# A small marker transfer that holds back one key load in a DMA-bound attention decode kernel

## The chip, the cores and the metric

One core of a Trainium2 chip. The metric is the device time of the whole program in microseconds (us), the median of several executions. The core was alone. A "ratio" below is worked out from runs of the same rounds, so it isn't quite the ratio of the medians that stand beside it. "Span" is the length of the one profiled execution, about 2 us shorter than its device time.

## The reference

Two attention layers, A and B, decode one token for four batch entries; their results are concatenated.

```python
# per layer: x (4, 1, 512), caches (4, 8, 8192, 128), wq (512, 4096), wo (4096, 512), bf16
q = (x @ wq) -> (4, 32, 1, 128)
k, v = caches, each of 8 heads used by 4 query heads   # B: only the last 2048 tokens
p = softmax(q k^T * 128 ** -0.5)
layer = (p v) -> (4, 1, 4096) @ wo
out = concatenate([A, B], axis=-1)                     # (4, 1, 1024)
```

## The kernel before

The work is cut into 20 units: four of layer B and sixteen of layer A (two heads of one batch entry each). An A unit loads 4 MB of keys and 4 MB of values into one of two slots, transposes the keys on TensorE, computes scores, the softmax and the weighted sum. From unit 6 on, every second unit also brings in 1 MB of the output weights, called a piece. SyncE issues all these loads, each behind the wait that frees its buffer. The part that matters (cuts are marked with ...):

```python
def kv_load(kind, u):
    ...
    w = [("otr", u - 2)] if kind == "V" else [("otr", u - 3)] if u >= 2 * T0P else [("T", tjob_idx[(u - 2, NJ - 1)])]
    ...
    op("sp", lambda sp: sp.sem_inc(sem, bump), waits=w, bump=(sem, bump, None))
    ...
    op("sp", dma(buf[:, slot, :, :].rearrange("p t d -> p (t d)"), src), inc=(kind, u, 0))
...
for u in range(1, NU + 1):
    if u < NU:
        kv_load("K", u)
    kv_load("V", u - 1)
    tn = u // 2
    if u % 2 == 0 and tn in pieces:
        P, q = pieces[tn]
        src = WO[P][q * C * DH:(q + 1) * C * DH, :].rearrange("(p r) n -> p (r n)", p=128)
        op("sp", dma(Wo_sb[:, :, :].rearrange("p r n -> p (r n)"), src), waits=[("ocp", tn - 1)], inc=("wo", tn))
```

So the order around the first piece is: keys of unit 6, values of unit 5, the piece, keys of unit 7, values of unit 6, keys of unit 8.

## Time and profile before

| | before |
|---|---|
| median device time | 439.15 us (3 runs, 438.97 to 439.83) |
| span of the profiled run | 437.0 us |
| bytes read | 184.56 MB |
| TensorE busy | 365.0 us (84%) |
| share of the 16 DMA engines' time in SyncE's queue | 99.1% |

The first thing to read is which resource has no free time. That is the DMA queue; the lines stand in the prediction. The second is what each of the sixteen DMA engines does by itself, and no single line of the page says that. I took it from the completion increments in the trace: a transfer over 128 partitions leaves sixteen of them, one per engine. In the text below, an engine's "lead" is how long before the last engine it finished the same transfer, "spread" is the greatest lead, a "straggler" is one engine well behind all others, and "lands" means the last increment. The profile doesn't number the engines: that two packets ran on the same one is read from the second starting where the first ends.

### The profile page before, as it was taken

Reading aid. Unit: us, or ns where it says so; the run is one execution under the profiler, and the core shown is the slowest. Engines: PE = TensorE matmul, PEld = TensorE weight load, DVE = VectorE, ACT = ScalarE, POOL = GpSimd, SP = SyncE. Lnnn points to the kernel's source line nnn. Section 1 sums busy time; section 2 is a strip of 40 time slices with the busy share of each in tenths; the row PEclk is TensorE's granted clock in tenths of the full one; section 3 lists DMA queues with packets and bytes.
Section 4 is the critical chain, followed back from the end, with each engine's and each line's share of the span. In section 5 each row is a group of like instructions: output and inputs, shape, how many; then the busy total and the mean of one; then the engine's idle time right before and its main releaser. Section 6 shows DMA issues by size and latency. Waiting matters only on the chain.

```text
span 437.0 us, 15525 instructions
## 1 busy us (share of the span) xinstructions
PE 365.0 (84%) x7174; PEld 337.9 (77%) x7184; DVE 210.0 (48%) x406; ACT 195.0 (45%) x249; POOL 27.7 (6%) x88
## 2 busy tenths in 40 slices
PE   0168898998998959895989598969868996989996
PEld 0158897997997949795979588868868886979975
DVE  0004455664564634563456247525643563455651
ACT  1024473573653625371634254434534462536530
POOL 6100000000000000000000000000100000000000
PEclk9999999999999988999999899989996999799999
DMA  8999999999999999999999999999999999999996
GB/s 340 430 421 421 429 412 430 418 439 412 445 432 432 424 438 432 432 432 432 432 432 429 432 432 430 431 433 432 410 454 432 432 432 432 432 432 411 447 407 255
DMA packets 10996, 184.73 MB, mean 423 GB/s; under 512 B 1236, under 2 KB 2280, under 8 KB 2408
## 3 DMA queue, kind: packets, MB, share of 16 engines
q1 hardware_dynamic: 10960, 184.56, 99.1%
q8 instruction: 8, 0.13, 0.1%
q14 instruction: 4, 0.03, 0.0%
q10 hardware_dynamic: 24, 0.01, 0.0%
HBM read 184.56 MB, written 0.01 MB: 422 GB/s over the span
## 4 chain that ended last, share of the span: by engine, by line
PE 54%; DMA 40%; issue 2%; DVE 1%; SPq 1%; ACT 1%
DMA K_sb<-in_A_k_cache_dram 29%; PE KT L283 27%; PE OT L338 11%; DMA K_sb<-in_B_k_cache_dram 7%; PE SB L322 5%; PE SA L322 4%; DMA V_sb<-in_A_v_cache_dram 4%; PE KT L396 4%; PE SA L350 1%; PE KT L338 1%; SPq L566 1%; DVE oacc L404 1%; PE KT L263 1%; ACT KT_sb L299 1%; DVE OS L501 0%
## 5 line engine op out<-in xcount | busy, mean ns | idle before, releaser
L283 PE MATMUL KT<-identf,K_sb 128*128 128x128 f32 x1280 | 207.6, 296 | 44.1 <-DMA K_sb<-in_A_k_cache_dram 30.7
L299 ACT ACTIVATE KT_sb<-KT 128x1024 bf16<-128x1024 bf16 (+1 forms) x192 | 165.1, 881 | 120.6 <-PE KT L283 120.6
L283 PEld LDWEIGHTS KT<-identf,K_sb 128*128 128x128 f32 x1280 | 147.6, 150 | 49.3 <-DMA K_sb<-in_A_k_cache_dram 31.7
L299 DVE COPY KT_sb<-KT 128x512 int32<-128x512 int32 x160 | 110.5, 691 | 132.1 <-PE KT L283 130.7
L338 PE MATMUL OT<-PT,V_sb 128*128 128x64 bf16 x2560 | 78.1, 193 | 1.6 <-issue 1.1
L338 PEld LDWEIGHTS OT<-PT,V_sb 128*128 128x128 bf16 x2560 | 75.9, 98 | 1.8 <-issue 1.2
L469 ACT ACTIVATE PT<-Dt 128x512 bf16<-128x512 f32 x40 | 24.6, 630 | 84.0 <-DVE Dt L458 84.0
L322 PEld LDWEIGHTS SA<-RQc,KT_sb 128*128 128x128 bf16 x1280 | 56.9, 98 | 2.3
L322 PEld LDWEIGHTS SB<-RQc,KT_sb 128*128 128x128 bf16 x1280 | 51.1, 97 | 7.9 <-issue 4.4
L322 PE MATMUL SA<-RQc,KT_sb 128*128 128x16 bf16 x1280 | 56.4, 170 | 0.0
L322 PE MATMUL SB<-RQc,KT_sb 128*128 128x16 bf16 x1280 | 52.9, 170 | 0.0
L420 DVE TENSOR_REDUCE M<-SB 128x8 f32<-128x512 f32 (+1 forms) x20 | 13.8, 692 | 50.0 <-PE SB L322 50.0
L441 POOL PARTITION_ALL_REDUCE MB<-M1m x20 | 7.7, 387 | 334.3 <-DVE M1m L434 334.3
L396 PE MATMUL KT<-Wo_sb,OL 128*4 128x512 bf16 x80 | 18.9, 379 | 0.0
L201 PE MATMUL KT<-ident,x_sb 4*128 4x4 bf16 x8 | 0.6, 170 | 19.9 <-POOL identf L537 19.9
L201 PEld LDWEIGHTS KT<-ident,x_sb 4*128 4x128 bf16 x8 | 0.4, 112 | 20.1 <-issue 20.1
L476 DVE TENSOR_REDUCE LB<-SA 128x8 f32<-128x512 f32 (+1 forms) x20 | 13.7, 684 | 2.8 <-PE SA L350 2.8
L458 DVE TENSOR_TENSOR Dt<-SA,MBm 128x512 f32<-128x512 f32 x20 | 13.8, 692 | 0.7
L367 DVE TENSOR_TENSOR ORx<-KT,MSK 32x1024 bf16<-32x1024 bf16 x10 | 12.1, 1211 | 3.3 <-PE KT L362 3.3
L458 DVE TENSOR_TENSOR Dt<-SB,MBm 128x512 f32<-128x512 f32 x20 | 13.6, 681 | 0.0
L420 DVE TENSOR_REDUCE M<-SA 128x8 f32<-128x512 f32 (+1 forms) x20 | 13.6, 681 | 0.0
L350 PE MATMUL SA<-PT,onesb 128*128 128x128 bf16 x168 | 12.7, 218 | 0.0
(69 smaller groups left out, 118.0 us busy)
## 6 DMA issues: line engine op xcount, KB each, us to landing
K_sb<-in_A_k_cache_dram SPq DMA_DIRECT2D x15, 4096.0 KB, 22.5
V_sb<-in_A_v_cache_dram SPq DMA_DIRECT2D x15, 4096.0 KB, 30.3
K_sb<-in_B_k_cache_dram SPq DMA_DIRECT2D x8, 2048.0 KB, 23.6
V_sb<-in_B_v_cache_dram SPq DMA_DIRECT2D x16, 1024.0 KB, 18.4
V_sb<-in_B_wq_dram SPq DMA_DIRECT2D x1, 4096.0 KB, 12.5
V_sb<-in_A_wq_dram SPq DMA_DIRECT2D x1, 4096.0 KB, 21.8
Wo_sb<-in_B_wo_dram SPq DMA_DIRECT2D x4, 1024.0 KB, 11.9
K_sb<-in_A_k_cache_dram SPq DMA_DIRECT2D x2, 2048.0 KB, 17.5
```

The source lines that it names most:

```text
L283: ins = pe.transpose(out=bkf[:, pi * 128:(pi + 1) * 128], in_=K_sbf[:, slot, t0:t0 + 2, :].rearrange("p t d -> p (t d)"), identity=identf[ ...
L299: ins = e.tensor_copy(out=d, in_=r) if eng == "dve" else e.activation(out=d, in_=r, func=ACTF.Copy)
L322: ins = pe.matmul(out=stb[:, t % NTH * C:(t % NTH + 2) * C], lhsT=ktv[:, pi, :, e], rhs=RQc[:, u % 2, t // TS, e, :], start=(e == 0), stop ...
L338: ins = pe.matmul(out=otb[:, s * NW:s * NW + w], lhsT=V_sb[:, slot, t, :], rhs=PT[:, slot, t * C:t * C + w], start=(j == 0), stop=(j == n ...
L350: ins = pe.matmul(out=SA[u % 2][:, s * NM:(s + 1) * NM], lhsT=onesb[:, :], rhs=PT[:, u % 2, c0:c0 + NM], start=(i == 0), stop=(i == n - 1))
L367: return dve.tensor_tensor(out=ORx[:, :, :, :], in0=bk[0:NR, 0:128].rearrange("p (i o r) -> p r o i", o=1, r=C).broadcast_to([NR, C, C, 12 ...
L396: ins = pe.matmul(out=bk[0:Bn, 0:D], lhsT=OL[:, i, :], rhs=Wo_sb[:, i, :], start=(i == 0), stop=(i == C - 1))
L420: return dve.tensor_reduce(out=M1[:, h * n:(h + 1) * n].rearrange("p (s h) -> p s h", h=C), in_=bank[:, :].rearrange("p (s j h) -> p s h j ...
L441: return pool.partition_all_reduce(MB[:, 0:n], M1m[:, 0:n], channels=128, reduce_op=ReduceOp.max)
L458: return dve.tensor_tensor(out=Dt[:, h * NTH * C:(h + 1) * NTH * C].rearrange("p (s j h) -> p s j h", s=Sh, h=C), in0=bank[:, :].rearrange ...
L469: return act.activation(out=PT[:, u % 2, a:b], in_=Dt[:, a:b], func=ACTF.Exp, scale=scale)
L476: return dve.tensor_reduce(out=LB[:, 0:n].rearrange("p (s h) -> p s h", h=C), in_=SA[u % 2][:, 0:NSEG * NM].rearrange("p (s j h) -> p s h ...
```

## The change

Ahead of the first output weight piece, SyncE issues a 1 KB load into a scratch tile, the marker. The key load behind the piece (keys of unit 7) waits until the marker has landed, that is until every DMA engine has worked off all that was queued before. What then still lies in the queue behind the marker is called the "cover" below: it keeps the engines busy until the keys begin to flow. Here it is the piece, 2.5 us of work. The names in the code ("rs", "passed") and the place suggest the intent: bring the sixteen engines level again.

```diff
+        MARKS = (5,)
+        marked = []
+        def mark(u):
+            if u in MARKS:
+                op("sp", dma(rs_sb[:, :], WO[0][0:16, 0:32]), inc=("rs", u))
+                marked.append(u)
+        def passed():
+            return [("rs", marked.pop())] if marked else []
 ...
             w = [("otr", u - 2)] if kind == "V" else ...
+            if kind == "K":
+                w = w + passed()
 ...
             if u % 2 == 0 and tn in pieces:
                 P, q = pieces[tn]
+                mark(u - 1)
                 src = WO[P][...]
```

The rest of the diff is the scratch tile, the semaphore, and the same two calls in the branch for layer B's units, which do nothing with `MARKS = (5,)`.

More of the change, by code (lines that the diff above doesn't have):

```diff
@@ L120, in bass_concat_heads__gqa_block_cached__sliding_block_cached__decode_kernel @@
         osb = sb("osb", [Bn, 2, D], BF16)
+        rs_sb = sb("rs_sb", [16, 32], BF16)
         dummy = sb("dummy_t", [128, 2], F32)
@@ L128, in bass_concat_heads__gqa_block_cached__sliding_block_cached__decode_kernel @@
                  "out0", "out1", "out2", "Tq", "Td", "Ta", "S", "PV", "Ed", "Ea", "Eq", "vs", "sub", "exp", "otr", "otp",
-                 "ocp", "Ef", "fin0", "fin1", "ar1", "SM", "msk", "pset", "setup", "pm0", "pm1", "oc", "ocB", "mkb", "perm", "rq"]
+                 "ocp", "Ef", "fin0", "fin1", "ar1", "SM", "msk", "pset", "setup", "pm0", "pm1", "oc", "ocB", "mkb", "perm", "rq", "rs"]
         sems = {n: sm("s_" + n) for n in names}
@@ L160, in sem_of @@
             return sems["vs" if t in ("max", "maxc", "sum", "rcp", "os") else t]
-        DMA_KEYS = ("K", "Kh", "KH", "V", "Vh", "VL", "WL", "x", "out", "WQ", "wo")
+        DMA_KEYS = ("K", "Kh", "KH", "V", "Vh", "VL", "WL", "x", "out", "WQ", "wo", "rs")
         plan = {e: [] for e in ("sp", "pe", "act", "dve", "pool")}
@@ L720, in kv_load @@
                     if kind == "K":
-                        w = [("T", tjob_idx[(u - 2, 8 * q + 7)])] if u >= 2 else []
+                        w = ([("T", tjob_idx[(u - 2, 8 * q + 7)])] if u >= 2 else []) + passed()
                     else:
                         w = [("otr", u - 2)] if u >= 2 else [("T", tjob_idx[(1, 1)])] if u else [("T", qp_idx[(1, NQP - 1)])]
+                        if q == NSEG - 1:
+                            mark(u)
                     heads = HKV // NPART[kind]
```

## The prediction

> **What bounds the kernel now.** I read the page's busy shares first, then its slices, then SyncE's timeline around the one place that changes, and last the chain of waits there. From the page:
>
> ```profile
> PE 365.0 (84%) x7174; PEld 337.9 (77%) x7184; DVE 210.0 (48%) x406; ACT 195.0 (45%) x249; POOL 27.7 (6%) x88
> ...
> DMA  8999999999999999999999999999999999999996
> ...
> q1 hardware_dynamic: 10960, 184.56, 99.1%
> ...
> HBM read 184.56 MB, written 0.01 MB: 422 GB/s over the span
> ```
>
> The sixteen DMA engines are busy in every slice but the first and the last, and SyncE's queue takes 99.1% of their time; no other engine passes 84%. So the kernel ends when 184.56 MB have passed, plus a short tail. What counts in any change is whether one of the sixteen engines, the last one above all, runs dry.
>
> SyncE's timeline, 120 to 165 us (start, duration, what was issued):
>
> ```profile
> 124.63 0.55 SPq L566 DMA_DIRECT2D V_sb<-in_A_v_cache_dram  x1
> 140.94 0.34 SPq L566 DMA_DIRECT2D Wo_sb<-in_B_wo_dram  x1
> 141.46 0.53 SPq L566 DMA_DIRECT2D K_sb<-in_A_k_cache_dram  x1
> 142.10 0.55 SPq L566 DMA_DIRECT2D V_sb<-in_A_v_cache_dram  x1
> 159.25 0.54 SPq L566 DMA_DIRECT2D K_sb<-in_A_k_cache_dram  x1
> ```
>
> These are V of unit 5, the first output weight piece, K of unit 7, V of unit 6 and K of unit 8. The chain in order of time says when this K lands and who wants it:
>
> ```profile
> 141.46 22.50 DMA K_sb<-in_A_k_cache_dram
> 163.96 0.04 issue
> 164.00 3.68 PE KT L283 x16
> ```
>
> K of unit 7 is issued at 141.46 but lands at 163.96 only, because it queues behind V of unit 5. That V, alone in its window, took
>
> ```profile
> DMA to landing us min/median/max: 27.1/27.1/27.1
> ```
>
> so it lands at 124.63 + 27.1 = 151.75. The same view gives the weight piece 13.3 us, so it lands at 140.94 + 13.3 = 154.25. TensorE waits up to 5.3 us for such keys (the view of waits, longest of its row), so a late K is passed on to TensorE at once. The end is the DMA's too: the last piece of weights lands at 434.43 and the last matmul ends 0.4 us later.
>
> **The sixteen engines are not level.** Each transfer leaves sixteen completion increments in the trace, one per engine. For V of unit 5 the lead of each engine over the last one was, in us: 2.07 2.01 1.73 1.58 1.38 1.35 1.30 0.57 0.41 0.39 0.34 0.31 0.26 0.11 0.08 0.00. For the first transfer of the run the greatest lead was 0.80; it reached 2.11 at 54 us and stays at 2.05 to 2.11 until the final weights. The steps down of single engines fall on instruction fetches: a fetch of 8 or 16 KB takes a place on one engine and costs it some 0.6 us (the one at 159.8 us takes a lead of 1.30 to 0.67). Packets of 32 KB take 1.21 us on every engine, 27 GB/s each.
>
> **What the Trainium skill says.**
> - "DMA: Bandwidth & Descriptors", section "Queues, rings and completion order": on one DMA engine descriptors are consumed in ring order, and the increment lands only after that engine's earlier writes. So the marker passes when V of unit 5 has drained. The trace agrees: landings come in the order of issue.
> - Same page, section "Why a DMA increments its semaphore by 16 and not by 1": the number of engines is the largest k up to 16 dividing both slowest dimensions. The marker has 16 partitions, so it has one 64-byte row on each of the 16 engines, and its full count means that the last engine has passed. No run here shows it yet.
> - Same page, section "Where 436 GB/s comes from": a ceiling of 435.2 GB/s. The slices of the middle show 429 to 434, so there is no reserve of rate from which a gap could be made good.
> - "Perfetto Trace Analysis", section "DMA Instruction — HWDGE (DVE, Sync)": an issue's start is when its waits are satisfied, and the data movement lies after it. The trace agrees: 0.54 us of issue, then many us to landing.
>
> **The change, part by part.** It removes nothing and moves no bytes but 1 KB. Only mark 5 is in the list, so there is one marker.
> - The marker's issue: no wait; it goes out right after V of unit 5, near 125.2 us, where SyncE is idle until 140.94. About 0.35 us of issue, all hidden.
> - The marker's data: per engine one row of 64 bytes and one increment. Packets of 1 KB took 0.044 us and increments 0.009 us in the trace. At most 0.05 us of each engine's time, on the path.
> - The weight piece stays at 140.94 (it waits for a DVE result). Its rows now lie behind the marker: 154.25 - 151.75 = 2.50 us of work on each engine.
> - K of unit 7 waits. The marker lands on the last engine at about 151.75 + 0.05 = 151.80. SyncE wakes in 0.02 to 0.05 us and does the same few semaphore steps that now take 141.46 - 141.28 = 0.18 us, part of them before the wait. Issue at about 151.95, which is 10.5 us later than now. V of unit 6 follows at 152.6 instead of 142.1. K of unit 8 waits for a result at 159.25 either way, so SyncE is back in step.
> - The question is whether 2.50 us of weights cover the restart of the queue. The only transfer that starts on an empty queue is the first one. The page's table of issues:
>
> ```profile
> V_sb<-in_B_wq_dram SPq DMA_DIRECT2D x1, 4096.0 KB, 12.5
> V_sb<-in_A_wq_dram SPq DMA_DIRECT2D x1, 4096.0 KB, 21.8
> ```
>
> Issued at 0.80 and 1.24, they land at 13.32 and 23.00. So 4 MB in a running queue takes 9.68 us, and from an empty one 12.52: 2.84 us of restart on the last engine, 2.0 on the first (its increment came 0.80 earlier). Its first packets began 1.04 to 1.6 us after the issue (one at 2.1) and took 1.7 to 2.2 us instead of 1.21.
> - Gap on the last engine = (issue after the last landing) 0.20 + (restart) 2.0 to 2.84 - (cover) 2.50 = -0.3 to +0.54 us. Taken as a whole, K would land by 151.95 + 12.52 = 164.47 at the latest against 163.96 now: 0.5 us later. If the last engine never runs quite dry, it lands at 164.0. I put 0.3.
> - The engines in front do run dry, for up to 1.3 us, and lose their lead. That alone costs nothing. But the lead is a cushion: of the fetches after 152 us (159.8, 289.1, 431.3 us) each costs its engine some 0.6 us, and now the leads are perhaps 0.3 to 0.8, so one such engine may become the new last by up to 0.3 us. These don't add, as they fall on different engines. I put 0.1.
>
> Sum: 439.15 + 0.3 + 0.1 = 439.55, and since the queue never holds fewer than several us of work elsewhere and runs at its ceiling, what is lost at 152 us stays lost to the end.
>
> **The rivals.**
> - Levelling helps. The intent is plainly to bring the engines level. If the last engine could use what the leading ones give up, the most to gain is the mean lead, 13.9 / 16 = 0.87 us, hence 438.3. Against it: leads stay constant to 0.05 us over 300 us, so engines don't share one pool; each runs at its own 27 GB/s and nothing that the fast ones leave reaches the slow one.
> - The cover is far too short. If a restart in mid-run cost more than at the start (the memory is under load), or the marker came back later than I think, the whole queue stands still by 1 to 3 us: 440.5 to 442. For it: the first packets after an empty queue are half as long again. Against it: the queue isn't empty, the weights still flow on the late engines.
> - The gap is hidden. K lands when it did, and fetches fall on engines with enough lead: 439.15, no change at all. This is nearly as likely as my sum, and the three runs of before (438.97 to 439.83) spread more than the difference.
> - TensorE takes over as the bound: not with the change of one wait, as TensorE idles before the keys of each pair of units.
>
> **Range and chances.** Low end 438.7: levelling helps by half of its most, or the run-to-run scatter goes down. High end 440.6: a full gap of 0.54, a fetch of 0.3 to 0.6 and the scatter. 2% is 8.8 us, three times what the worst rival makes: within 2% by 98%, each side 1%.
>
> **What the profile after would show.** Right: a marker issue near 125.2 us; K of unit 7 issued at 151.7 to 152.2; its increments spread 0.4 to 0.9 us instead of 2.10, and the spread stays small; K of unit 7 landing between 163.9 and 164.6; every later landing shifted by the same amount; the DMA's slice near 153 us a little under full. Wrong: a K landing under 163.8 with later landings that gain on the old ones (levelling helps), a landing over 165 (the cover is too short), or a spread that stays at 2.1 (the marker doesn't hold the leaders back).

## The result

The changed kernel took 441.23 us (6 runs, 440.69 to 441.7), the kernel before 439.19 us in the same rounds; ratio 1.0044, 95% interval 1.0031 to 1.0057. That is 2.0 us slower. It stays within 2%, but it is five times the 0.4 us that I had forecast, and it lies above my range.

The page of the profile after:

```profile
span 439.0 us, 15526 instructions
...
q1 hardware_dynamic: 10992, 184.56, 98.8%
```

The same bytes take 2.0 us more of span, and SyncE's queue has 98.8% of the engines' time in place of 99.1%. SyncE's timeline after, 120 to 180 us (start, duration, what was issued):

```profile
124.84 0.55 SPq L567 DMA_DIRECT2D V_sb<-in_A_v_cache_dram  x1
125.44 0.58 SPq L567 DMA_DIRECT2D rs_sb<-in_A_wo_dram  x1
141.16 0.35 SPq L567 DMA_DIRECT2D Wo_sb<-in_B_wo_dram  x1
152.26 0.54 SPq L567 DMA_DIRECT2D K_sb<-in_A_k_cache_dram  x1
152.90 0.54 SPq L567 DMA_DIRECT2D V_sb<-in_A_v_cache_dram  x1
159.44 0.54 SPq L567 DMA_DIRECT2D K_sb<-in_A_k_cache_dram  x1
```

Here the reader sees the hold: the piece goes out at 141.16 as before, and the keys of unit 7 follow only at 152.26. By 159.44 SyncE is back in step. The chain of waits after, in the same place:

```profile
125.44 26.75 DMA rs_sb<-in_A_wo_dram
152.19 0.02 SPq L757
152.21 0.05 issue
152.26 12.80 DMA K_sb<-in_A_k_cache_dram
165.05 0.05 issue
165.10 3.67 PE KT L284 x16
```

The marker lands at 152.19, SyncE issues the keys 0.07 us later, and they land at 165.05. Before, it was 163.96. The stretch from 152 to 156 us, of the kernel before and then of the changed one (length, busy time of each engine, granted clock, DMA share, GB/s; packets count where they start):

```profile
152.00:156.00 4.00, 3.93 (x98) 3.62 (x98) 1.60 (x4) 1.83 (x2) 0.00 (x0) 1.00 1.10 469
```

```profile
152.00:156.00 4.00, 3.93 (x97) 3.62 (x95) 1.45 (x3) 2.02 (x2) 0.00 (x0) 1.00 0.99 354
```

469 GB/s against 354: the DMA engines had a hole there. TensorE passes it on. Its waits for keys between 120 and 190 us (total, times, longest), before and then after:

```profile
PE KT L283 <- DMA K_sb<-in_A_k_cache_dram: 6.9, 2, 5.3
```

```profile
PE KT L284 <- DMA K_sb<-in_A_k_cache_dram: 7.8, 2, 6.2
```

The hole is only half of the loss. Following the landings of the same transfers through both traces (after less before, us) gives a staircase:

| where | landing before | landing after | later by | new part |
|---|---|---|---|---|
| first weight piece | 154.25 | 154.41 | 0.17 | 0.17, there before the hold |
| keys of unit 7 | 163.96 | 165.05 | 1.09 | 0.93 |
| first of the eight last weight loads | 432.05 | 433.23 | 1.18 | 0.08 over 268 us |
| second of them | 432.40 | 434.41 | 2.01 | 0.83 |
| last of them | 434.43 | 436.44 | 2.01 | 0 |

(Columns are rounded separately, so 0.17 and 0.93 make 1.09. 0.05 of the 0.08 came at one landing, 298.87.)

The second large step is at the very end, 280 us after the only thing that was changed. The chains of waits of the end show it too; before, and then after:

```profile
426.70 0.38 issue
...
433.83 0.11 PE KT L700
```

```profile
412.20 22.21 DMA Wl_sb<-in_A_wo_dram
434.41 0.04 issue
434.46 0.27 PE KT L701
```

Before, the chain stays on TensorE from 426.70 on and passes through the final products without a stop. After, it hangs on the second weight load, which lands at 434.41.

What happened there can be read from two lists. Instruction fetches stand in the trace as packets of 8 KB on queue 14 and of 16 KB on queue 8. From 150 us to the last weights there are three: at 159.8, 289.1 (8 KB each) and 431.3 us (16 KB) before, at 160.4, 289.2 and 432.2 us after. Each takes a place on one DMA engine. And the leads around the last one are, in us:

```
before, 4th last weight load  2.02 1.75 1.52 1.33 1.30 1.29 0.61 0.56 0.42 0.35 0.35 0.29 0.20 0.12 0.05 0
before, 6th                   1.93 1.44 1.25 1.23 1.20 0.57 0.52 0.39 0.33 0.31 0.28 0.21 0.18 0.10 0.04 0
after, 1st last weight load   0.85 0.77 0.76 0.75 0.74 0.73 0.72 0.71 0.71 0.69 0.61 0.60 0.51 0.34 0.02 0
after, 2nd                    1.65 1.58 1.57 1.56 1.55 1.54 1.53 1.53 1.50 1.42 1.41 1.32 1.18 0.84 0.82 0
```

Before, the lead of 1.75 is gone in the second list and one of 0.21 is new, while the others barely move: one engine lost about 1.5 us and is still not the last, so nobody waits. After, all leads grow by 0.8 and one of 0.71 is missing: its engine lost the same 1.5 us and came out 0.8 us behind all others. That is the 0.83 us step of the table. The packets agree: the fetch lasts from 432.17 to 433.30, and the seven 1 KB packets that follow on its engine take 0.10 to 0.13 us instead of 0.046, as the seven behind the same fetch do before. The first step holds such a loss too. The fetch packet at 160.443 is followed on its engine by a key packet that starts at 160.749 and takes 1.43 us instead of 1.21. That engine finishes the keys of unit 7 last, 0.37 us behind the next. So 0.93 = 0.56 of restart gap on the engines in general + 0.37 from the fetch. The fetch at 289.2 us is the 0.05: the lists around it have one lead of about 0.65 less, and its engine came out last by 0.05 us.

This split is of one profiled execution. Three runs below have the same code up to this point (two markers, seven markers, extra load with the marker). In their traces the keys of unit 7 landed 11.02, 11.28 and 11.39 us after the piece, against 10.64 here and 9.71 in the kernel before. So the first step measured 0.93 to 1.68 us over four builds: it has no fixed size.

### The profile page after: what moved, and what is told of

Read it like the earlier page. It is cut to its first block, busy times and chain, and to the rows that moved or that the text cites. A ratio compares the mean times of both kernels' runs of the same rounds, so it can differ in the third digit from the quotient of the medians.

```text
span 439.0 us, 15526 instructions
## 1 busy us (share of the span) xinstructions
PE 366.3 (83%) x7174; PEld 338.1 (77%) x7184; DVE 209.9 (48%) x406; ACT 194.9 (44%) x249; POOL 27.6 (6%) x88
## 3 DMA queue, kind: packets, MB, share of 16 engines
q1 hardware_dynamic: 10992, 184.56, 98.8%
## 4 chain that ended last, share of the span: by engine, by line
PE 45%; DMA 45%; PEld 4%; issue 2%; SPq 2%; DVE 1%; ACT 0%; PEldq 0%
DMA K_sb<-in_A_k_cache_dram 26%; PE KT L284 23%; PE OT L339 9%; DMA K_sb<-in_B_k_cache_dram 7%; DMA rs_sb<-in_A_wo_dram 6%; DMA Wl_sb<-in_A_wo_dram 5%; PE SB L323 4%; PE SA L323 4%; PE KT L397 3%; PEld KT L284 2%; SPq L567 2%; PE SA L351 1%; DVE oacc L405 1%; PEld OT L339 1%; PEld SA L323 1%
## 5 line engine op out<-in xcount | busy, mean ns | idle before, releaser
L351 PE MATMUL SA<-PT,onesb 128*128 128x128 bf16 x168 | 12.8, 218 | 0.0
## 6 DMA issues: line engine op xcount, KB each, us to landing
V_sb<-in_B_wq_dram SPq DMA_DIRECT2D x1, 4096.0 KB, 12.2
```

The lines of the kernel that those rows point to most:

```text
L351: ins = pe.matmul(out=SA[u % 2][:, s * NM:(s + 1) * NM], lhsT=onesb[:, :], rhs=PT[:, u % 2, c0:c0 + NM], start=(i == 0), stop=(i == n - 1))
```

## The experiments

Theory after the result: the hold costs twice. First, the queue's restart isn't covered quite long enough and even the last engine has a gap. Second, the hold takes the leads of the other engines, and these had been absorbing the instruction fetches. Rivals: the marker's small rows disturb the queue; any wait of SyncE on a marker costs this; the gap is the whole cost and the rest is chance; the engines share one pool of bandwidth, so leads mean nothing.

All edits are against the changed kernel. All results were correct. A hold without a marker, waiting on the values' own semaphore, could not be built: TensorE's loop takes that semaphore down again on each pass, and the program asserts that no other engine waits on it.

**Marker without the hold.** The wait moves to a load that is issued after 159 us in any case.

```diff
-            if kind == "K":
+            if kind == "K" and u != 7:
                 w = w + passed()
```

> The marker goes out as in the changed kernel, but K of unit 7 doesn't wait for it; K of unit 8, which is issued after 159 us anyway, takes the wait. Theory (the hold costs a restart gap on the last DMA engine and the leads of the others; the marker itself costs 0.02 us): 439.2 us, K of unit 7 lands near 164.0, spread of its increments 2.1 us. Rival (the marker's small rows disturb the queue): 440 us or more.

Measured: 439.07 us against 439.28 before, ratio 1.0001 (0.9987 to 1.0015). The keys of unit 7 landed at 163.94, spread 2.12 us. The marker itself is free; the rival of disturbing rows is out, and the cost is the hold's.

**Marker and hold, 9.7 us more cover.** The marker goes out ahead of the values of unit 5 (`tn_of(u)` is `u // 2`).

```diff
+            if u % 2 == 0 and tn_of(u) in pieces:
+                mark(u - 1)
             kv_load("V", u - 1)
 ...
-                mark(u - 1)
                 src = WO[P][...]
```

> Marker and wait stay, but the marker goes before V of unit 5 instead of behind it, so that 9.7 us more of queued work cover the restart: K of unit 7 is issued near 142.4 us. Theory: no engine runs dry, leads stay at 2.1 us, 439.2 us. Rival (any wait of SyncE on a marker costs what the change costs): 441 us.

Measured: 439.32 us against 439.28, ratio 1.0001 (0.9987 to 1.0014). SyncE's timeline has the key load at

```profile
142.91 0.54 SPq L567 DMA_DIRECT2D K_sb<-in_A_k_cache_dram  x1
```

right after its marker landed at 142.83, so the wait was real. The keys landed 9.71 us after the piece, exactly as before, and the spread stayed at 2.57 us. Waiting on a marker cost nothing with this much work queued behind it.

**Cover of 4.9 us and of 3.7 us.** The values of unit 5 are cut in two transfers with the marker between (96 of 128 rows ahead of it, then 112).

```diff
+            cut = 96 if kind == "V" and u in MARKS else None
 ...
+            if cut is not None:
+                for i, (t0, t1) in enumerate(((0, cut), (cut, NT))):
+                    ...
+                    op("sp", dma(buf[:, slot, t0:t1, :]...), inc=("Vh", u, 9) if i == 0 else (kind, u, 0))
+                    if i == 0:
+                        mark(u)
+                return
 ...
-                mark(u - 1)
```

> V of unit 5 in two transfers, three quarters and one quarter, the marker between: cover 2.5 + 2.4 = 4.9 us. From the marker's last packet to streaming keys took 2.8 to 3.05 us in the changed kernel, so the last engine has no gap and only engines that lead by more than 1.9 us lose a little. Theory: 439.3 us, spread after K of unit 7 about 1.9 us. Rival (cost doesn't depend on cover): 441 us.

Measured: 439.21 us against 439.28, ratio 1.0003 (0.999 to 1.0017). The keys landed 9.72 us after the piece, spread 2.07. As the theory says.

> The same with seven eighths and one eighth: cover 3.7 us. No gap on the last engine, but every lead is cut to about 0.65 us. Theory (lead is a cushion for instruction fetches): K of unit 7 lands with the kernel before's time, the end is 0.4 to 0.9 us late, through the fetch near 432 us: 439.6 to 440.1 us. Rival (the gap is the whole cost): 439.2 us.

Measured: 439.98 us against 439.28, ratio 1.0018 (1.0004 to 1.0032). The chain of waits:

```profile
151.21 13.38 DMA K_sb<-in_A_k_cache_dram
164.59 0.04 issue
```

The piece had landed at 154.66, so the keys came 9.93 us later: a gap of 0.22 us, where I had expected none. The spread fell from 2.45 to 1.22 us (I had expected 0.65). At the end another 0.37 us went: the fetched engine led by 1.16 us and lost 1.5. The gap alone (0.22) doesn't make the 0.7 us. Gap and end, with 0.1 us that the split values and the marker took longer than the values of the kernel before (9.81 against 9.71), do. The leads matter.

**No cover.** The marker goes behind the piece.

```diff
-                mark(u - 1)
                 src = WO[P][...]
                 op("sp", dma(Wo_sb...), waits=[("ocp", tn - 1)], inc=("wo", tn))
+                mark(u - 1)
```

> The marker goes behind the weight piece, so nothing covers the restart of the queue. Theory: the last engine stands still for the whole restart of 2.8 to 3.05 us instead of 0.35 to 0.55, so 2.5 us more than the changed kernel: 443.6 us, K of unit 7 lands near 167.3, spread under 0.5 us. Rival (a large part of the loss comes from elsewhere and is not additive): under 442.5 us.

Measured: 443.62 us against 439.13, ratio 1.0104 (1.0089 to 1.0119). The chain:

```profile
141.38 13.12 DMA rs_sb<-in_A_wo_dram
...
154.57 12.81 DMA K_sb<-in_A_k_cache_dram
167.38 0.04 issue
```

2.4 us more than the changed kernel, for 2.5 us less cover: between these two the loss is one for one. From 3.7 to 2.5 us of cover it isn't quite: the gap grew by 0.71 for 1.2, and 0.37 of the larger gap was the fetch. The keys landed 12.81 us after the issue, against the 12.52 of the run's first transfer that I had worked from. The spread stayed 0.79 us, with one engine last by 0.43 (the one that the fetch at 160.3 us hit), so my "under 0.5" failed by that one.

**The hold at the last piece instead of the first.**

```diff
-        MARKS = (5,)
+        MARKS = (17,)
```

> The one marker at the last weight piece instead of the first. Theory: a gap of 0.4 to 0.6 us there, no fetch at 160 and 289 us on levelled engines, but the one near 432 us finds them level: its engine had led by 1.4 us before, now by 0.5 or less, cost 0.8 less that lead: 439.2 + 0.5 + 0.3 to 0.8 = 440.0 to 440.5 us. Rival (the whole cost arises at the hold and is the same wherever it is): 441.2 us.

Measured: 441.31 us against 439.13, ratio 1.0049 (1.0036 to 1.0062). My number was too low; the rival's 441.2 fits it, but the trace does not fit the rival. The two halves of the last keys follow a piece here, and the first half landed 5.40 us after it, against 4.90 before: a gap of 0.50 at the hold. Until the values at 422 us nothing more was lost. Then the fetch at 431.5 us hit an engine with a lead of at most 0.3 us, and the next landing came 2.71 us after the one before it instead of 1.33. I had put that fetch at 0.8 us; on an engine without a lead it costs some 1.4. So the whole cost does not arise at the hold; the sum is the same by chance.

**One engine loaded on purpose.** An extra load of 17 rows of 4 KB, issued behind the second piece, in the kernel without and with the marker.

```diff
+            if u == 8:
+                op("sp", dma(xt_sb[:, :], bass.AP(..., ap=[[2048, 17], [1, 2048]])), inc=("xt", 0))
```

> No marker, no hold; one extra load of 17 rows of 4 KB after V of unit 7, which runs on one DMA engine alone: about 17 x 0.155 = 2.65 us of that engine's time. Theory (a lead is a cushion): only one lead falls, by about 2.65 us, and every later landing is late by 2.65 us less the lead that this engine had, which is 0 to 2.1 us; so 439.7 to 441.9 us, and the trace says which. Rival (the engines share one pool of bandwidth): 70 KB spread over sixteen, 0.2 us, 439.4 us.

Measured: 442.13 us against 439.21, ratio 1.0067 (1.0054 to 1.008), just above the range that I gave. The trace has the 17 packets one after another, from 194.12 to 197.97: 3.85 us of one engine, more than the 2.65 I had worked out, as the later packets took up to 0.37 us instead of 0.16. The engine had a lead of 1.16 us (this lead is missing from the list after it). 3.85 - 1.16 = 2.69; the next keys landed 2.90 us late, 0.2 more than that, which stays unexplained, and it stayed so to the end. Spread over a pool it would have been 0.2 us. One engine's work in excess of its lead becomes the kernel's time.

> The same extra load in the changed kernel. Theory: the levelled engine has 0.4 to 0.7 us of lead, so the landings fall back by 1.9 to 2.2 us at the extra load; the fetch near 432 us, on another engine, then costs nothing more: 441.2 - 0.8 + 2.0 = 442.4 us (443.3 if the fetch hits the same engine). Rival (one pool): 441.4 us.

Measured: 443.29 us against 439.21, ratio 1.0096 (1.0082 to 1.0111). I had expected 442.4. The other number that I gave, 443.3, fits, but not for its reason: the extra load and the last fetch did not add up here. In this run the first hold had left one engine far behind the rest, so the loaded engine had a lead of about 1.65 us and not 0.7; the landings fell back by 2.48 us (3.86 - 1.65 = 2.2). With 1.67 us lost at the first hold this makes 4.15, against 4.1 measured. (The fetch at 160.1 us hit another engine than the straggler and cost nothing.) The last fetch cost nothing more, since the other engines led the straggler by 1.6 us and more.

**More than one hold.**

```diff
-        MARKS = (5,)
+        MARKS = (5, 7, 9, 11, 13, 15, 17)
```

> A marker and a hold at each of the seven weight pieces. Theory: each hold leaves a gap of 0.4 to 0.6 us on the last engine, the lost cushion costs once: 439.2 + 7 x 0.5 + 1.2 = 443.9 us. Rival (levelling is a one-time cost, level engines lose nothing more): 441.2 us.

Measured: 452.2 us in six executions. The longest, 456.28, lies 1.5% above the fastest and counts as slow; without it 452.0 (449.42 to 453.59) against 439.13, ratio of the fast runs 1.0289 (1.0263 to 1.0316). Nearly three times the forecast loss, with about five times the usual scatter. Both theories missed it. In its trace the keys behind the seven pieces came late by 1.57, 2.88, 2.22, 1.07, 0.58, 1.70 and 0 us. At the second, fifteen engines began their keys at 196.15 to 196.84 and one at 198.69, which then stood 2.4 us behind. One engine still had 0.7 us of the piece to do when the others had finished; that it is the same one isn't shown.

> Markers at the first and second weight piece, to see what a second hold costs on engines that are level already; seven holds cost 13 us instead of the 4.7 expected. If holds are additive at the first one's gap: 441.7 us. If a hold on level engines costs more (1.8 us each, (452.2 - 441.2) / 6): 443.0 us, and one engine alone stands out by 1.5 to 2.5 us at the second hold, starting its keys late though they were issued long before.

Measured with two holds: 442.02 us (441.71 to 443.73) against 439.21, ratio 1.0072 (1.0057 to 1.0086). The time lies between the two expectations. In the trace the second hold cost 1.70 us, again with one engine alone behind, by 1.2 us. So the second expectation has the straggler, but not its size (1.5 to 2.5) and not its late start: it began at 197.09, the others from 196.03 to 197.03, and its first packet took 2.43 us. With a straggler of that size fourteen of the others had their cushion back, and the last fetch cost only 0.1 us instead of 0.8.

> All seven markers and holds, each V before a weight piece split so that a quarter of it lies behind the marker: cover 4.9 us each. Theory (all the cost of the seven holds is restart with too little cover): 439.5 us or less than 1 us above it, leads stay near 2 us. Rival (late issue as such, seven times, lets SyncE or the queue fall behind): 445 us or more.

Measured with all seven holds and 4.9 us of cover at each: 439.9 us against 439.21, ratio 1.0018 (1.0005 to 1.0031). The keys land 9.71 us after the first piece and the spread is still 1.9 us at the end. Of the 12.9 us that the seven holds had cost (452.0 - 439.13) 0.7 are left, and the split itself makes them: the values that were cut in two took 0.1 us more each. So the loss of the seven holds, stragglers included, is a matter of restarting with too little queued. Why one engine restarts up to 2 us after the others, or takes twice as long for its first packet, though its keys were issued in the same instruction, stays open.

The terms side by side. "Gap" is keys less piece, against 9.71 (4.90 for the last marker); "end" is how much the stretch from the last full value load to the last weights grew over the 12.63 us of the kernel before. Gap and end are of one profiled execution each:

| kernel | cover, us | gap at the hold | end | time less before |
|---|---|---|---|---|
| marker, no hold | - | 0 | 0 | -0.2 |
| marker ahead of the values | 12.2 | 0 | -0.1 | 0.0 |
| a quarter behind | 4.9 | 0 | 0 | -0.1 |
| an eighth behind | 3.7 | 0.2 | 0.4 | 0.7 |
| the change | 2.5 | 0.9 | 0.8 | 2.0 |
| last piece only | 2.5 | 0.5 | 1.3 | 2.2 |
| marker behind the piece | 0 | 3.4 | 0.8 | 4.5 |

## Why the prediction was wrong

- **Bound, place and direction: right.** The kernel is DMA-bound, the hold is the only part that costs, what is lost there isn't made good, and levelling brings no gain. After the hold the leads are as constant as in the kernel before: 0.7 us of spread from 165 to 289 us.
- **The issue time: right, a little early.** Keys at 152.26, predicted about 151.95. Of the difference 0.25 us is a later start of the whole run (values of unit 5 landed 152.00). The rest is a marker that landed 0.19 us after the values and not 0.05, less an issue that followed it in 0.07 us and not 0.15.
- **"Gap on the last engine = ... -0.3 to +0.54 us ... I put 0.3": mis-sized.** It was 0.56 us without the fetch, just above the upper end, and in two other runs with the same first hold the gap without the fetch was larger: 0.86 us with two markers (1.31 less the 0.45 by which the fetched engine was last) and 1.68 where the extra load follows. The form of the term (restart less cover) held; a straggler at the restart was not in it. From the marker's last packet at 151.50 to the keys it was 0.69 us to the landing, 0.07 to the issue, 1.32 to 1.57 to most engines' first packets; those packets ended at 155.53 to 155.76, some 0.7 us later than packets that start in a running queue. The two engines still at work began at 154.19 and 154.40, the other fourteen by 153.83.
- **"each costs its engine some 0.6 us, and now the leads are perhaps 0.3 to 0.8, so one such engine may become the new last by up to 0.3 us. These don't add ... I put 0.1": this step failed.** The mechanism was named and the leads were guessed well (0.37 to 0.70), but the three fetches cost 0.37 + 0.05 + 0.83 = 1.25 us of kernel time and not 0.1. Two parts were wrong. The last fetch costs about 1.5 us and not 0.6. "8 or 16 KB ... some 0.6 us" was a misreading of the trace before: its 8 KB fetches cost about 0.65 (at 90.9, 159.8 and 289.1 us), its 16 KB fetches at 51.2, 70.8 and 431.3 us about 1.5 (leads of 1.46 to 0, 1.69 to 0.13, 1.75 to 0.21). I took the size from the one at 159.8. And the losses did add, although they fell on different engines: each was larger than the lead that its engine had over the engine that was then the last (at 432 us 1.53 against 0.71).
- **The range.** Its high end added one gap, one fetch of up to 0.6 and scatter. Two fetches at 1.2 us together were not in it. The sum of the terms is 0.56 + 0.37 + 0.83 + 0.08 (0.05 of it the fetch at 289 us) = 1.84, and with the 0.17 us of start-up the 2.0 us of span.
- **The signs named for "wrong".** A landing over 165 was named as the sign of too little cover, and came (165.05; 0.17 of it is start-up). The spread of 0.4 to 0.9 came (0.70). "Every later landing shifted by the same amount" held within 0.1 us until 432 us and failed there.
- **Rivals.** Levelling as a gain didn't show in any run. The runs with 4.9 us of cover and more are the "hidden gap" rival made real. "The cover is far too short", 440.5 to 442 us, has the measured 441.23 in its range, in part by luck: the restart alone cost 0.56 us in that trace and not 1 to 3, and a like amount came at the end. In other runs with the same hold the restart did cost over 1 us.
- **Two loose readings.** "The slices of the middle show 429 to 434" passes over a pair of 410 and 454, and the spread from 54 us to the final weights runs from 2.03 to 2.13, not from 2.05 to 2.11. Neither carries the result.

What is shown: the hold and not the marker costs; the gap follows the cover; an engine's extra work beyond its lead becomes time. That the end step is the fetch is read from traces: in each of five (before, the change, an eighth behind, last piece only, marker behind the piece) a 16 KB fetch packet of 0.97 to 1.13 us is followed on its engine by seven slow 1 KB packets, and one engine loses some 1.4 to 1.6 us at that place. Moving the fetch itself wasn't tried. No version faster than the kernel before was found.

## What to carry to other kernels

Here sixteen DMA engines ran one queue without a pause. The last of them set the time, and the leads of the others weren't waste: they absorbed instruction fetches and other single-engine work at no cost. If a load has to wait for a point in the queue, place that point far enough ahead: here 4.9 us of queued work behind the marker made the wait free, 3.7 us cost 0.7 and 2.5 us cost 2.0. And a cost measured at one event (0.6 us for an 8 KB fetch) shouldn't be put on another of twice the size (1.5 us) without looking.

## What the Trainium skill lacked or had wrong

- "Runtime: NRT & Kernel Launch", section "Instruction fetch mechanics", gives blocks of 16 KiB, which agrees with the packets on queue 8 here (those on queue 14 are of 8 KB), and calls the fetch hidden by the sequencer's pace. It lacks the other side: in a DMA-bound kernel a fetch takes a place on one DMA engine. Here 8 KB cost that engine about 0.6 us and 16 KB about 1.5 us, and what goes beyond the engine's lead is kernel time (0.37 and 0.83 us in the changed kernel).
- No page read for this case has the lasting leads among the sixteen engines: 2.0 to 2.1 us of spread from 54 us to the final weights in the kernel before.
- "DMA: Bandwidth & Descriptors", section "Latency and other measured facts", has about 600 ns to the first byte on the SyncE and ScalarE path. The two 2 KB stores at the end took 0.76 us from the start of the issue to the first packet (ScalarE's 435.18 to 435.94, SyncE's 435.33 to 436.09). For a 4 MB load behind the hold it was 1.32 to 1.57 us to the first packet on most engines, and up to 2.1 us on the two that were still at work. It has no figure for what a restart of this path behind a wait costs in all: with the marker behind the piece, 4 MB from an empty queue took 12.8 us (0.4 of it a fetch) against 9.7 in a running one, so about 2.7 us.
